# Other token blocks and the other operand standing in a two-product layer on Trainium2

## The chip, the cores and the metric

The kernel runs on one core of a Trainium2 chip. Its time is the device time of one execution, in microseconds (us); a version is judged by the median of several executions. The work of a core is done by TensorE (PE, matrix products, with PEld for its weight loads), VectorE (DVE), ScalarE (ACT), GpSimd (POOL) and SyncE (SP, whose queue issues the DMAs here).

## The reference

Attention with a cap on its scores, and then a layer of two matrix products with a gate between them:

```python
scores = cap * tanh(q @ k.T / sqrt(64) / cap)          # batch 4, 12 heads, 448 tokens, head size 64
attn   = softmax(scores);  x = attn @ v                # x: 1792 tokens x 768
h = x @ w_in                                           # 768 x 2048
g = h * cos(h)
out = g @ w_out                                        # 2048 x 768, out: 1792 x 768
```

## The kernel before

**Attention** runs in 12 cycles of three head pairs each, in an order written out by hand: a list of parts with due times (`PLAN`, a cycle of 13.8 us), sorted into one sequence. It leaves `x` in SBUF, split into a high and a low part (`xh`, `xl`, type fp32r), with the model dimension on the partitions and the tokens along the free axis. In its last cycle it already begins the layers: `BEGIN` places the first product of two units (`layers.begin`, into banks of the tile `pair`), and `layers.first` does most of the first unit's elementwise work there.

**The layers** are cut into 8 groups (`NGRP`) of 256 hidden columns, that is two units of 128 (`GF = 2`), and each group into 4 blocks of 448 tokens (`S`), one for each batch. A group and block is a step, 32 in all. Products are made of three terms, high x high, low x high and high x low, so 18 matmuls make a unit's first product (6 chunks of the model dimension, line 196: 128 columns of `w_in` stand, 448 tokens move). In the second product (line 601) 128 columns of `w_out` stand and 448 tokens of the gated values move: for each of the 6 chunks of output rows 2 units x 3 terms, 36 matmuls a block.

`Layers.step` is the written order of a step. On PE: both units' first products of this block, then the second product of the block before (`prev`), in three bank pairs; the first two come from the tile `pair` (two buffers of two banks), the third is `rest` (one buffer). On ACT and DVE: a piece of the weights of a later group is taken from 64-bit to fp32r words (`magnitude` on ACT; `clamp`, `shift`, `tail_bits`, `sign_bit` on DVE, lines 231 to 256; `high` on ACT and `low` on GpSimd in the next step); each unit passes through `turns` (ACT, 558), `whole_turns` (DVE, 561), `reduce` (two on DVE, 566 and 567), `cosine` (ACT, 570), `gate` (DVE, 573), `high` (ACT, 576) and `low` (DVE, 579); and the sums of `prev` are added from PSUM to `acc` in SBUF (DVE, 613; a copy in the first group, 611). The third chunk's addition is left to the next step (`older`). In the last group each addition is followed by its output DMA on SP's queue (616). The output leaves with the model dimension first, and the host transposes it.

Of the kernel before, what the change touches and what calls it, by code (L numbers as in the profile page):

```python
# [22 lines left out]
DM = H * D  # L23
DFF = 2048
KC = DM // 128
NF = DFF // 128
NG = 4
NQUAD = NPAIR // 2
# [46 lines left out]
EARLY = [2, 4, 6, 8]  # L75
EARLY_AT = dict(no_sign=2.4, scale=2.9, cap=3.4, shift=3.9, tail_bits=16.2, sign_bit=17.1, load=17.2, high=18.1, low=19.8, load_rest=20.0)
BUSY = 6, 5
PAD = 144
KD = 512
QK = KD + S  # L80
Q = slice(KD, QK)
# [23 lines left out]
@with_exitstack  # L105
def attention_moe(ctx: ExitStack, tc: tile.TileContext, qkv, cap, w_in, w_out, out):
    nc = tc.nc
    const = ctx.enter_context(tc.tile_pool(name="const", bufs=1))

    with tc.manual_schedule():  # L110
        busy = const.tile([128, 512], BF16, name="busy")
        nc.vector.memset(busy, 0.0)
        with tc.tile_pool(name="first", bufs=1, space=PSUM) as pool:
            keep_busy(nc, pool.tile([128, 512], F32, name="idle"), busy, BUSY[0])
        capt = const.tile([128, 1], F32, name="capt")
        nc.sync.dma_start(out=capt, in_=cap.rearrange("(a b) -> a b", b=1).to_broadcast([128, 1]))
        w64 = const.tile([128, DM, 2], I32, name="w64")
        u = const.tile([128, DM], I32, name="u")
        raw = w64.bitcast(F32).rearrange("p a b -> p (a b)")[:, 0:QK]
        for h in (slice(0, 64), slice(64, 128)):  # L120
            nc.sync.dma_start(out=raw[h], in_=qkv[0, h, 0:QK])
        second = const.tile([128, QK], F32, name="second")
        nc.sync.dma_start(out=second, in_=qkv[1, :, 0:QK])
        nc.sync.dma_start(out=u.bitcast(F32)[:, 0:RAW - QK], in_=qkv[0, :, QK:RAW])
        cabs = const.tile([128, PAD], F32, name="cabs")[:, 0:1]
        nc.scalar.activation(cabs, capt, AF.Abs)  # L126
        inv = const.tile([128, 1], F32, name="inv")
        nc.vector.reciprocal(inv, capt)
        nc.vector.tensor_scalar_mul(inv, inv, 1.0 / math.sqrt(D))
        bits = nc.values_load(cabs[0:1, 0:1].bitcast(I32))  # L130
        with tc.If(bits < CAP_LIMIT_BITS) as cmp:
            body(tc, w64, u, second, busy, qkv, capt, inv, w_in, w_out, out, True)
        with cmp.Else():
            body(tc, w64, u, second, busy, qkv, capt, inv, w_in, w_out, out, False)


def body(tc, w64, u, second, busy, qkv, capt, inv, w_in, w_out, out, bounded):
    with ExitStack() as ctx:
        xp = ctx.enter_context(tc.tile_pool(name="xp", bufs=1))
        xh = xp.tile([128, NPAIR, NT], F32R, name="xh")  # L140
        xl = xp.tile([128, NPAIR, NT], F32R, name="xl")
        wts = Weights(tc, w64, u, w_in, w_out)
        angles = xp.tile([128, 128], F32, name="angles")
        tc.nc.gpsimd.memset(angles[:, 0:1], math.pi / 2)
        tc.nc.gpsimd.memset(angles[:, 1:2], 0.25)
        wts.open_in(xp, (0, 1))
        wts.open_in(xp, (0,), "wo")
        banks = Banks(ctx.enter_context(tc.tile_pool(name="banks", bufs=2, space=PSUM)))
        keep_busy(tc.nc, banks.rest()[:, 1], busy, BUSY[1])
        layers = Layers(tc, banks, wts, xh, xl, angles, out)  # L150
        with ExitStack() as actx:
            if bounded:
                attention(actx, tc, banks, second, qkv, capt, inv, xh, xl, wts, layers, xp)
            else:
                attention_general(actx, tc, banks, qkv, capt, inv, xh, xl)
                for f in (0, 1):
                    wts.whole("wi", f)
                wts.whole("wo", 0)
                wts.load("wo", 1)
                wts.words()  # L160
                wts.load("wi", 2)
                for j in range(GF):
                    layers.begin(j)
                layers.sine()
        with ExitStack() as mctx:
            layers.open(mctx)
            layers.run()
# [21 lines left out]

def hidden(nc, wts, f, xh, xl, h, b):  # L190
    hi, lo = wts.get("wi", f)
    toks = slice(S * b, S * b + S)
    for k in range(KC):
        ks = slice(128 * k, 128 * k + 128)
        for i, (w, x) in enumerate(terms(f // GF, hi, lo, xh, xl)):
            nc.tensor.matmul(h[:, 0:S], lhsT=w[:, ks], rhs=x[:, k, toks],  # L196
                             start=(k == 0 and i == 0), stop=(k == KC - 1 and i == 2))


# [271 lines left out]
        eng.tensor_copy(out, in_)  # L471


def attention(ctx, tc, banks, second, qkv, capt, inv, xh, xl, wts, layers, pool):
    nc = tc.nc
    a = Heads(ctx, tc, banks, qkv, capt, inv, xh, xl, True)
    a.first(wts.w64.bitcast(F32).rearrange("p a b -> p (a b)")[:, 0:QK], second, wts.u.bitcast(F32)[:, 0:RAW - QK])
    a.fill()
    todo = []

# [6 lines left out]
    for j, time in enumerate(BEGIN):  # L487
        at(CYCLE * (NQ - 1) + time, lambda j=j: layers.begin(j))
    at(CYCLE * (NQ - 1) + FIRST, layers.sine)
    at(CYCLE * (NQ - 1) + FIRST, lambda: layers.first(pool))  # L490
    pieces = (("wi", 0), ("wi", 1), ("wo", 0), ("wo", 1), ("wi", 2))
    at(CYCLE + 4.0, lambda: wts.load(*pieces[0]))
    for i, cycle in enumerate(EARLY):
# [40 lines left out]
GF = 2  # L534
# [4 lines left out]
class Unit:  # L539


    def __init__(self, m, f, j, b):
        self.m, self.f, self.j, self.b = m, f, j, b
        self.h, self.gone = None, ()

    def product(self, bank=None):
        if self.h is None:
            h = bank if bank is not None else self.m.banks.single()
            hidden(self.m.nc, self.m.wts, self.f, self.m.xh, self.m.xl, h, self.b)
            self.h = h[:, 0:S]  # L550

    def tile(self, name):
        return self.pool.tile([128, S], F32, name=name, tag=name)

    def turns(self):
        m = self.m
# [16 lines left out]
        self.m.nc.vector.tensor_mul(self.y, self.h, self.y)  # L573

    def high(self):
        self.m.nc.scalar.copy(self.g[0][:, self.j], self.y)  # L576

    def low(self):
        self.m.nc.vector.tensor_sub(self.g[1][:, self.j], self.y, self.g[0][:, self.j])  # L579


class Block:


    def __init__(self, m, G, b, g):
        self.m, self.G, self.b, self.g = m, G, b, g
        self.y = {}

    def last(self, i):
        return self.G == NGRP - 1 and self.b == B - 1 and i == 2  # L590

    def product(self, i):
        m = self.m
        y = self.y[i] = m.banks.product(i)
        gh, gl = self.g
        for e in range(2):
            c = slice(128 * (2 * i + e), 128 * (2 * i + e) + 128)
            for j in range(GF):
                hi, lo = m.wts.get("wo", GF * self.G + j)
                for k, (w, x) in enumerate(terms(self.G, hi, lo, gh, gl)):  # L600
                    m.nc.tensor.matmul(y[:, e, 0:S], lhsT=w[:, c], rhs=x[:, j],  # L601
                                       start=(j == 0 and k == 0), stop=(j == GF - 1 and k == 2))

    def add(self, i):
        m, y = self.m, self.y.pop(i)
        toks = slice(S * self.b, S * self.b + S)
        parts = [slice(0, 1), slice(1, 2)] if self.last(i) else [slice(0, 2)]
        for e in parts:
            acc = m.acc[:, 2 * i + e.start:2 * i + e.stop, toks]
            if self.G == 0:  # L610
                m.nc.vector.tensor_copy(acc, y[:, e, 0:S])
            else:
                m.nc.vector.tensor_add(acc, y[:, e, 0:S], acc)  # L613
            if self.G == NGRP - 1:
                rows = m.out[128 * (2 * i + e.start):128 * (2 * i + e.stop), toks]
                m.nc.sync.dma_start(out=rows.rearrange("(e p) t -> p e t", p=128), in_=acc)


class Layers:
# [14 lines left out]
    def sine(self):  # L634
        self.nc.scalar.activation(self.angles[:, 2:3], self.angles[:, 1:2], AF.Sin)

    def first(self, pool):

        unit = self.begun[0]
        unit.pool, unit.gone = pool, ("turns", "whole_turns", "reduce", "cosine", "gate")  # L640
        for part in unit.gone:
            getattr(unit, part)()

    def open(self, ctx):
# [2 lines left out]
        accp = ctx.enter_context(self.tc.tile_pool(name="m_acc", bufs=1))  # L647
        self.wts.open_in(accp, (2, 3))
        self.wts.open_in(accp, (1, 2), "wo")
        self.acc = accp.tile([128, KC, NT], F32, name="acc")  # L650

    def run(self):
        prev, older = None, None
# [3 lines left out]
    def step(self, step, prev, older):  # L657
# [2 lines left out]
        piece = self.todo.pop(0) if self.todo else None  # L660
        units, cur = [], None
        if step < NSTEP:
            g = [self.gp.tile([128, GF, S], F32R, name=nm, tag=nm) for nm in ("gh", "gl")]
            units = [Unit(self, GF * G + j, j, b) for j in range(GF)] if step else self.begun
            for unit in units:
                unit.pool, unit.g = self.vp, g
# [8 lines left out]
                getattr(units[j], part)()  # L675

        def add(block, i):
            if block is not None:
                block.add(i)

        if self.done:
            wts.high(*self.done)
            wts.low(*self.done)
        on(0, "product")
        on(1, "product")
        if prev is not None:
            for i in range(3):
                prev.product(i)
        add(older, 2)
        on(0, "turns")  # L690
        w("magnitude")
        w("clamp")
        w("shift")
        on(0, "whole_turns")
        on(0, "reduce")
        on(0, "cosine")
        w("tail_bits")
        on(0, "gate")
        on(0, "high")
        w("sign_bit")  # L700
        on(1, "turns")
        on(0, "low")
        on(1, "whole_turns")
        on(1, "reduce")
        on(1, "cosine")
        add(prev, 0)
        on(1, "gate")
        on(1, "high")
        add(prev, 1)
        on(1, "low")  # L710
        if step == NSTEP:
            add(prev, 2)
        self.done = piece
        if self.todo and step:
            wts.load(*self.todo[0])
# [1 line left out]


_INS = ['qkv', 'cap', 'w_in', 'w_out']
_OUTS = [((DM, NT), 'float32')]  # L720


def _layout(inputs):
# [46 lines left out]
```

## Time and profile before

| | us |
|---|---|
| median of 3 runs (lowest, highest) | 664.13 (663.76, 664.15) |
| the profiled execution's own time | 664.33 |
| its span, first to last instruction | 662.5 |
| PE busy, share of the span | 651.9, 98% |
| DVE busy | 493.8, 75% |
| ACT busy | 318.1, 48% |
| POOL busy | 62.0, 9% |

The span is what the profile's rows cover; the profiled execution is 1.8 us longer than its span, and 0.20 us above the median. Rows of the timeline and of the chain count from the span's start. Records of matmuls overlap, so a matmul's record is longer than the time from its start to the next matmul's start.

### The profile page before, as it was taken

How to read it: one execution, taken by the hardware profiler on the slowest of the kernel's cores; microseconds unless marked ns; L12 is line 12 of the kernel's file. 1: busy time of each engine (PE TensorE's matmuls, PEld its weight loads, DVE VectorE, ACT ScalarE, POOL GpSimd, SP SyncE). 2: the span in 40 equal slices, each digit the busy share in tenths (PEclk: the TensorE clock that was granted, in tenths of full speed). 3: DMA queues.
4: the chain of work that ended last, by engine and by line, in shares of the span. 5: the costliest groups of instructions: out<-in, count | busy, mean ns of one | idle time of the engine just before them, and what ended most of it. 6: DMA issues, size and time to landing. Idle time of an engine off the chain costs nothing.

```text
span 662.5 us, 8791 instructions
## 1 busy us (share of the span) xinstructions
PE 651.9 (98%) x3563; PEld 490.0 (74%) x3563; DVE 493.8 (75%) x739; ACT 318.1 (48%) x385; POOL 62.0 (9%) x39
## 2 busy tenths in 40 slices
PE   7999999999999999999999999999999999999996
PEld 2333333333489999999999999999999999999995
DVE  1599999997778876677777776677777776677663
ACT  4999999999724433333333333333333333333220
POOL 0001011000011111111111111111111121111000
PEclk9899999999999999999999999999999999999998
DMA  7044332542001211111112111111112111110224
GB/s 257 10 151 147 111 139 92 182 150 102 1 1 50 94 49 47 48 47 48 48 52 85 55 47 48 48 48 49 48 57 72 63 48 48 48 48 0 84 85 171
DMA packets 19616, 49.41 MB, mean 75 GB/s; under 512 B 2160, under 2 KB 5232, under 8 KB 19568
## 3 DMA queue, kind: packets, MB, share of 16 engines
q1 hardware_dynamic: 19568, 48.77, 21.8%
q8 instruction: 30, 0.49, 0.3%
q14 instruction: 18, 0.15, 0.1%
HBM read 43.25 MB, written 5.51 MB: 74 GB/s over the span
## 4 chain that ended last, share of the span: by engine, by line
PE 98%; ACT 1%; DMA 0%; issue 0%; DVE 0%
PE single L196 35%; PE pair L601 24%; PE rest L601 12%; PE single L421 12%; PE pair L328 9%; PE rest L337 3%; PE rest L430 2%; PE pair L196 1%; DMA capt<-in_cap_dram 0%; PE rest L102 0%; ACT t L362 0%; ACT late L347 0%; ACT t L347 0%; DVE acc L613 0%; ACT cabs L126 0%
## 5 line engine op out<-in xcount | busy, mean ns | idle before, releaser
L570 ACT ACTIVATE y<-y,angles 128x448 f32<-128x448 f32 x64 | 43.0, 672 | 149.4 <-DVE y L567 149.4
L558 ACT ACTIVATE v<-single,angles 128x448 f32<-128x448 f32 x62 | 39.2, 633 | 101.4 <-PE single L196 101.4
L246 DVE TENSOR_SCALAR u<-u 128x768 f32<-128x768 f32 x28 | 15.7, 561 | 94.9 <-ACT u L231 94.9
L613 DVE TENSOR_TENSOR acc<-pair,acc 128x896 f32<-128x896 f32 x56 | 60.6, 1083 | 3.9 <-PE pair L601 3.9
L576 ACT CAST gh<-y 128x448 fp32r<-128x448 f32 x64 | 36.3, 567 | 49.6 <-DVE y L573 49.6
L328 PE MATMUL pair<-qk 64*128 64x448 f32 x264 | 58.6, 562 | 0.0
L328 PEld LDWEIGHTS pair<-qk 64*128 64x128 f32 x264 | 22.7, 186 | 36.2 <-issue 20.1
L347 ACT ACTIVATE t<-pair,inv 128x896 f32<-128x896 f32 x48 | 45.9, 1004 | 6.0 <-PE pair L328 5.5
L579 DVE TENSOR_TENSOR gl<-y,gh 128x448 fp32r<-128x448 f32 x64 | 40.8, 638 | 4.0 <-ACT gh L576 4.0
L362 ACT ACTIVATE t<-t,capt 128x1792 f32<-128x1792 f32 x24 | 42.8, 1783 | 0.4
L401 DVE TENSOR_TENSOR sum<-t 128x896 f32<-128x896 f32 x24 | 26.1, 1088 | 21.9 <-ACT t L362 21.9
L567 DVE SCALAR_TENSOR_TENSOR y<-v,y 128x448 f32<-128x448 f32 x64 | 40.0, 625 | 2.2
L421 PE MATMUL single<-late,v 128*32 128x448 f32 x368 | 40.7, 542 | 0.0
L573 DVE TENSOR_TENSOR y<-single,y 128x448 f32<-128x448 f32 x62 | 38.2, 616 | 2.7 <-ACT y L570 2.7
L566 DVE SCALAR_TENSOR_TENSOR y<-v,single 128x448 f32<-128x448 f32 x62 | 38.5, 621 | 2.1
L421 PE MATMUL single<-t,v 128*32 128x448 f32 x368 | 39.4, 547 | 0.0
L601 PE MATMUL pair<-gh,wo0h 128*128 128x448 f32 x96 | 35.3, 368 | 0.0
L601 PE MATMUL pair<-gh,wo0l 128*128 128x448 f32 x96 | 35.3, 368 | 0.0
L601 PE MATMUL pair<-gl,wo0h 128*128 128x448 f32 x96 | 35.3, 368 | 0.0
L196 PE MATMUL single<-xl,wi2h 128*128 128x448 f32 x96 | 35.3, 368 | 0.0
L196 PE MATMUL single<-xh,wi2h 128*128 128x448 f32 x96 | 35.3, 368 | 0.0
L196 PE MATMUL single<-xh,wi2l 128*128 128x448 f32 x96 | 35.3, 368 | 0.0
(143 smaller groups left out, 1609.5 us busy)
## 6 DMA issues: line engine op xcount, KB each, us to landing
w<-in_w_in_dram SPq DMA_DIRECT2D x32, 384.0 KB, 3.6
w<-in_w_out_dram SPq DMA_DIRECT2D x32, 384.0 KB, 3.6
qk<-in_qkv_dram SPq DMA_DIRECT2D x22, 480.0 KB, 5.5
v<-in_qkv_dram SPq DMA_DIRECT2D x23, 256.0 KB, 4.0
out_dram<-acc SPq DMA_DIRECT2D x11, 448.0 KB, 2.5
w<-in_qkv_dram SPq DMA_DIRECT2D x2, 240.0 KB, 3.8
second<-in_qkv_dram SPq DMA_DIRECT2D x1, 480.0 KB, 5.7
out_dram<-acc SPq DMA_DIRECT2D x2, 224.0 KB, 2.8
```

The source lines that it names most:

```text
L196: nc.tensor.matmul(h[:, 0:S], lhsT=w[:, ks], rhs=x[:, k, toks], start=(k == 0 and i == 0), stop=(k == KC - 1 and i == 2))
L328: self.nc.tensor.matmul(ps[:, h, 0:S], lhsT=x[mine, 128 * g:128 * g + 128], rhs=x[mine, Q], start=True, stop=True)
L347: self.nc.scalar.activation(out, ps[:, :, 0:S], AF.Tanh, scale=self.inv)
L362: self.nc.scalar.activation(t, t, AF.Exp, scale=self.capt)
L421: self.nc.tensor.matmul(self.acc[q][e][o], lhsT=self.v[q, a][:, g, d], rhs=t, start=(g == first), stop=(g == last), tile_position=(0, o.st ...
L558: m.nc.scalar.activation(self.v, self.h, AF.Identity, bias=m.quarter, scale=1.0 / (2.0 * math.pi))
L566: m.nc.vector.scalar_tensor_tensor(self.y, self.v, -TWO_PI_HI, self.h, op0=ALU.mult, op1=ALU.add)
L567: m.nc.vector.scalar_tensor_tensor(self.y, self.v, -TWO_PI_LO, self.y, op0=ALU.mult, op1=ALU.add)
L570: self.m.nc.scalar.activation(self.y, self.y, AF.Sin, bias=self.m.half_pi)
L579: self.m.nc.vector.tensor_sub(self.g[1][:, self.j], self.y, self.g[0][:, self.j])
L601: m.nc.tensor.matmul(y[:, e, 0:S], lhsT=w[:, c], rhs=x[:, j], start=(j == 0 and k == 0), stop=(j == GF - 1 and k == 2))
L613: m.nc.vector.tensor_add(acc, y[:, e, 0:S], acc)
```

## The change

Token blocks are 512, 512, 384 and 384 (starting at 0, 512, 1024, 1408) instead of four of 448. In the second product 128 tokens of the gated values stand and 384 of the 768 columns of `w_out` move, the two halves one after the other with the same standing operand; a bank pair holds 128 tokens x 768, so a block has 4 or 3 chunks, and the fourth takes a buffer of `pair` again. `acc` and the output have the tokens first, and the host's transpose goes. The order of additions in a step changes: `magnitude` goes ahead of the first unit's `turns`; the first chunk's addition moves from behind the second unit's cosine to behind the first unit's low part (in step 1 to before `tail_bits`); a fourth chunk's addition is left to the next step as the third's is; in step 0 the second unit's `turns` goes first. Tiles of a unit are 512 wide; the first unit's scratch is the tile `second`, now 1,024 wide, which held a piece of attention's input, and `PAD` shrinks by the same 64 words.

```diff
+HALF = DM // 2
+BLOCKS = 512, 512, 384, 384
+STARTS = 0, 512, 1024, 1408
+WIDE = max(BLOCKS)
-PAD = 144
+PAD = 80
...
-        second = const.tile([128, QK], F32, name="second")
-        nc.sync.dma_start(out=second, in_=qkv[1, :, 0:QK])
+        second = const.tile([128, 1024], F32, name="second")
+        nc.sync.dma_start(out=second[:, 0:QK], in_=qkv[1, :, 0:QK])
...
-    toks = slice(S * b, S * b + S)
+    n = BLOCKS[b]
+    toks = slice(STARTS[b], STARTS[b] + n)
...
-            nc.tensor.matmul(h[:, 0:S], lhsT=w[:, ks], rhs=x[:, k, toks],
+            nc.tensor.matmul(h[:, 0:n], lhsT=w[:, ks], rhs=x[:, k, toks],
...
     def tile(self, name):
-        return self.pool.tile([128, S], F32, name=name, tag=name)
+        t = self.space[name] if self.space else self.pool.tile([128, WIDE], F32, name=name, tag=name)
+        return t[:, 0:BLOCKS[self.b]]
...
     def product(self, i):
         m = self.m
         y = self.y[i] = m.banks.product(i)
+        toks = slice(128 * i, 128 * i + 128)
         gh, gl = self.g
-        for e in range(2):
-            c = slice(128 * (2 * i + e), 128 * (2 * i + e) + 128)
-            for j in range(GF):
-                hi, lo = m.wts.get("wo", GF * self.G + j)
-                for k, (w, x) in enumerate(terms(self.G, hi, lo, gh, gl)):
-                    m.nc.tensor.matmul(y[:, e, 0:S], lhsT=w[:, c], rhs=x[:, j],
+        for j in range(GF):
+            hi, lo = m.wts.get("wo", GF * self.G + j)
+            for k, (w, x) in enumerate(terms(self.G, hi, lo, gh, gl)):
+                for e in range(2):
+                    m.nc.tensor.matmul(y[:, e, 0:HALF], lhsT=x[:, j, toks], rhs=w[:, HALF * e:HALF * e + HALF],
                                        start=(j == 0 and k == 0), stop=(j == GF - 1 and k == 2))
...
     def add(self, i):
-        toks = slice(S * self.b, S * self.b + S)
+        t = STARTS[self.b] // 128 + i
...
-            acc = m.acc[:, 2 * i + e.start:2 * i + e.stop, toks]
+            acc = m.acc[:, t, e]
...
-                rows = m.out[128 * (2 * i + e.start):128 * (2 * i + e.stop), toks]
-                m.nc.sync.dma_start(out=rows.rearrange("(e p) t -> p e t", p=128), in_=acc)
+                cols = slice(HALF * e.start, HALF * e.stop)
+                m.nc.sync.dma_start(out=m.out[128 * t:128 * t + 128, cols],
+                                    in_=acc.rearrange("p e n -> p (e n)"))
...
+        if step == 0:
+            units[1].turns()
+            units[1].gone = ("turns",)
...
         if prev is not None:
-            for i in range(3):
+            for i in range(prev.count):
                 prev.product(i)
         add(older, 2)
+        add(older, 3)
+        w("magnitude")
         on(0, "turns")
-        w("magnitude")
         w("clamp")
         w("shift")
         on(0, "whole_turns")
         on(0, "reduce")
         on(0, "cosine")
+        if step == 1:
+            add(prev, 0)
         w("tail_bits")
         on(0, "gate")
         on(0, "high")
         w("sign_bit")
         on(1, "turns")
         on(0, "low")
+        if step != 1:
+            add(prev, 0)
         on(1, "whole_turns")
         on(1, "reduce")
         on(1, "cosine")
-        add(prev, 0)
         on(1, "gate")
         on(1, "high")
         add(prev, 1)
         on(1, "low")
         if step == NSTEP:
             add(prev, 2)
+            add(prev, 3)
...
-    return _np.ascontiguousarray(got[0].T)
+    return got[0]
```

## Rows read from the trace of the kernel before

**Rows 1.** The page: busy time of PE, and the chain that ended last.

```profile
PE 651.9 (98%) x3563; PEld 490.0 (74%) x3563; DVE 493.8 (75%) x739; ACT 318.1 (48%) x385; POOL 62.0 (9%) x39
...
PE 98%; ACT 1%; DMA 0%; issue 0%; DVE 0%
```

**Rows 2.** The chain in order of time (start, length, what): begun units, one step.

```profile
175.63 3.83 PE pair L196 x18
...
183.36 3.91 PE pair L196 x18
...
440.24 7.44 PE single L196 x36
447.68 4.96 PE pair L601 x24
452.63 2.48 PE rest L601 x12
```

**Rows 3.** Windows, the layers stage: busy time of each engine, then granted clock, DMA.

```profile
187.10:655.80 468.70, 468.70 (x2269) 425.49 (x2267) 344.01 (x525) 158.59 (x247) 53.55 (x29) 1.00 0.17 56
```

**Rows 4.** Timeline (start, length, engine, line, operation): one matmul and load.

```profile
400.39 0.37 PE L196 MATMUL single<-xl,wi3h 128*128 128x448 f32 x1
400.40 0.19 PEld L196 LDWEIGHTS single<-xh,wi3h 128*128 128x128 f32 x1
```

**Rows 5.** Timeline of loads in attention, first and last of six groups.

```profile
103.10 0.13 PEld L421 LDWEIGHTS single<-t,v 128*32 128x32 f32 x4 [0.25 <-issue]
...
104.98 0.13 PEld L421 LDWEIGHTS single<-t,v 128*32 128x32 f32 x4 [0.24 <-issue]
```

**Rows 6.** Timeline of the first begun unit, loads, then matmuls.

```profile
175.56 0.19 PEld L196 LDWEIGHTS pair<-xh,wi0h 128*128 128x128 f32 x1 [0.73 <-ACT late L347]
175.67 0.19 PEld L196 LDWEIGHTS pair<-xh,wi0l 128*128 128x128 f32 x1
...
175.56 0.47 PE L196 MATMUL pair<-xh,wi0h 128*128 128x448 f32 x1
175.87 0.36 PE L196 MATMUL pair<-xh,wi0l 128*128 128x448 f32 x1
...
179.11 0.36 PE L196 MATMUL pair<-xl,wi0h 128*128 128x448 f32 x1
```

**Rows 7.** Busy-work at the start: group of all loads, then two in the timeline.

```profile
L102 PEld LDWEIGHTS <-busy 128*128 128x128 bf16 x11 | 1.4, 134 | 4.9 <-issue 3.7 <-DVE busy L112 1.2
...
1.59 0.15 PEld L102 LDWEIGHTS <-busy 128*128 128x128 bf16 x1 [0.28 <-issue]
...
2.87 0.15 PEld L102 LDWEIGHTS <-busy 128*128 128x128 bf16 x1 [0.28 <-issue]
```

**Rows 8.** Timeline of ACT and DVE in the step of rows 2.

```profile
444.53 0.88 ACT L231 ACTIVATE u<-w 128x768 f32<-128x768 f32 x1
445.44 0.56 DVE L246 TENSOR_SCALAR u<-u 128x768 f32<-128x768 f32 x1 [3.62 <-ACT u L231]
...
446.51 0.39 DVE L561 TENSOR_SCALAR v<-v 128x448 f32<-128x448 f32 x1
446.94 0.62 DVE L566 SCALAR_TENSOR_TENSOR y<-v,single 128x448 f32<-128x448 f32 x1
...
448.13 0.95 DVE L252 SCALAR_TENSOR_TENSOR u<-w,u 128x768 int32<-128x768 int32 x1
...
452.55 1.08 DVE L613 TENSOR_TENSOR acc<-pair,acc 128x896 f32<-128x896 f32 x1
```

**Rows 9.** Timeline: block 0's last low part, and the matmul that reads it.

```profile
194.69 0.63 DVE L579 TENSOR_TENSOR gl<-y,gh 128x448 fp32r<-128x448 f32 x1 [0.63 <-ACT gh L576]
...
195.59 0.37 PE L601 MATMUL pair<-gl,wo1h 128*128 128x448 f32 x1
```

**Rows 10.** Timeline of the end: last matmul, last additions.

```profile
655.63 0.37 PE L601 MATMUL rest<-gh,wo0l 128*128 128x448 f32 x1
656.03 1.16 DVE L613 TENSOR_TENSOR acc<-rest,acc 128x448 f32<-128x448 f32 x2 [1.39 <-PE rest L601]
```

More of the change, by code (lines that the diff above doesn't have):

```diff
@@ L152, in body @@
             if bounded:
-                attention(actx, tc, banks, second, qkv, capt, inv, xh, xl, wts, layers, xp)
+                attention(actx, tc, banks, second, qkv, capt, inv, xh, xl, wts, layers)
             else:
@@ L471, in copy, with attention @@
         eng.tensor_copy(out, in_)
-def attention(ctx, tc, banks, second, qkv, capt, inv, xh, xl, wts, layers, pool):
+def attention(ctx, tc, banks, second, qkv, capt, inv, xh, xl, wts, layers):
     nc = tc.nc
     a = Heads(ctx, tc, banks, qkv, capt, inv, xh, xl, True)
-    a.first(wts.w64.bitcast(F32).rearrange("p a b -> p (a b)")[:, 0:QK], second, wts.u.bitcast(F32)[:, 0:RAW - QK])
+    a.first(wts.w64.bitcast(F32).rearrange("p a b -> p (a b)")[:, 0:QK], second[:, 0:QK], wts.u.bitcast(F32)[:, 0:RAW - QK])
     a.fill()
@@ L489, in attention @@
     at(CYCLE * (NQ - 1) + FIRST, layers.sine)
-    at(CYCLE * (NQ - 1) + FIRST, lambda: layers.first(pool))
+    at(CYCLE * (NQ - 1) + FIRST, lambda: layers.first(second))
     pieces = (("wi", 0), ("wi", 1), ("wo", 0), ("wo", 1), ("wi", 2))
@@ L543, in __init__ @@
         self.m, self.f, self.j, self.b = m, f, j, b
-        self.h, self.gone = None, ()
+        self.h, self.gone, self.space = None, (), None
     def product(self, bank=None):
@@ L549, in product, with result @@
             hidden(self.m.nc, self.m.wts, self.f, self.m.xh, self.m.xl, h, self.b)
-            self.h = h[:, 0:S]
+            self.h = h[:, 0:BLOCKS[self.b]]
     def tile(self, name):
-        return self.pool.tile([128, S], F32, name=name, tag=name)
+        t = self.space[name] if self.space else self.pool.tile([128, WIDE], F32, name=name, tag=name)
+        return t[:, 0:BLOCKS[self.b]]
+    def result(self, part):
+        return self.g[part][:, self.j, 0:BLOCKS[self.b]]
     def turns(self):
@@ L575, in high @@
     def high(self):
-        self.m.nc.scalar.copy(self.g[0][:, self.j], self.y)
+        self.m.nc.scalar.copy(self.result(0), self.y)
     def low(self):
-        self.m.nc.vector.tensor_sub(self.g[1][:, self.j], self.y, self.g[0][:, self.j])
+        self.m.nc.vector.tensor_sub(self.result(1), self.y, self.result(0))
 class Block:
@@ L587, in __init__ @@
         self.y = {}
+        self.count = BLOCKS[b] // 128
     def last(self, i):
-        return self.G == NGRP - 1 and self.b == B - 1 and i == 2
+        return self.G == NGRP - 1 and self.b == B - 1 and i == self.count - 1
     def product(self, i):
@@ L605, in add @@
         m, y = self.m, self.y.pop(i)
-        toks = slice(S * self.b, S * self.b + S)
+        t = STARTS[self.b] // 128 + i
         parts = [slice(0, 1), slice(1, 2)] if self.last(i) else [slice(0, 2)]
         for e in parts:
-            acc = m.acc[:, 2 * i + e.start:2 * i + e.stop, toks]
+            acc = m.acc[:, t, e]
             if self.G == 0:
-                m.nc.vector.tensor_copy(acc, y[:, e, 0:S])
+                m.nc.vector.tensor_copy(acc, y[:, e, 0:HALF])
             else:
-                m.nc.vector.tensor_add(acc, y[:, e, 0:S], acc)
+                m.nc.vector.tensor_add(acc, y[:, e, 0:HALF], acc)
             if self.G == NGRP - 1:
-                rows = m.out[128 * (2 * i + e.start):128 * (2 * i + e.stop), toks]
-                m.nc.sync.dma_start(out=rows.rearrange("(e p) t -> p e t", p=128), in_=acc)
+                cols = slice(HALF * e.start, HALF * e.stop)
+                m.nc.sync.dma_start(out=m.out[128 * t:128 * t + 128, cols],
+                                    in_=acc.rearrange("p e n -> p (e n)"))
 class Layers:
@@ L635, in sine, with first @@
         self.nc.scalar.activation(self.angles[:, 2:3], self.angles[:, 1:2], AF.Sin)
-    def first(self, pool):
+    def first(self, space):
         unit = self.begun[0]
-        unit.pool, unit.gone = pool, ("turns", "whole_turns", "reduce", "cosine", "gate")
+        unit.space = {"v": space[:, 0:WIDE], "y": space[:, WIDE:2 * WIDE]}
+        unit.gone = ("turns", "whole_turns", "reduce", "cosine", "gate")
         for part in unit.gone:
@@ L649, in open @@
         self.wts.open_in(accp, (1, 2), "wo")
-        self.acc = accp.tile([128, KC, NT], F32, name="acc")
+        self.acc = accp.tile([128, NT // 128, 2, HALF], F32, name="acc")
     def run(self):
@@ L662, in step @@
         if step < NSTEP:
-            g = [self.gp.tile([128, GF, S], F32R, name=nm, tag=nm) for nm in ("gh", "gl")]
+            g = [self.gp.tile([128, GF, WIDE], F32R, name=nm, tag=nm) for nm in ("gh", "gl")]
             units = [Unit(self, GF * G + j, j, b) for j in range(GF)] if step else self.begun
@@ L677, in add @@
         def add(block, i):
-            if block is not None:
+            if block is not None and i < block.count:
                 block.add(i)
+        if step == 0:
+            units[1].turns()
+            units[1].gone = ("turns",)
         if self.done:
@@ L719 @@
 _INS = ['qkv', 'cap', 'w_in', 'w_out']
-_OUTS = [((DM, NT), 'float32')]
+_OUTS = [((NT, DM), 'float32')]
 def _layout(inputs):
```

## Prediction

> **What bounds the kernel now.** I read the page first. TensorE (PE) is busy for 98% of the span, and the chain that ended last is 98% PE. VectorE (DVE) has 75%, ScalarE (ACT) 48% [rows 1]. Busy PE alone proves little, since matmul records overlap, so I asked the chain in order of time. In the layers, one step repeats exactly: 36 matmuls of the first product in 7.44 us, 24 plus 12 of the second in 4.96 and 2.48, then the next step, with nothing between [rows 2]. A step is 14.88 us for 72 matmuls, 206.7 ns each, and over the whole layers stage (187.1 to 655.8, granted clock 1.00) 468.7 us stand for 2,268 starts, again 206.7 [rows 3]. So PE never waits there, and the time of this stage is (number of matmuls) x (time from one start to the next).
>
> The timeline of single matmuls says what those 206.7 ns are [rows 4]. At clock 1.00 (2.4 GHz) 448 columns stream in 448 / 2.4 = 186.7 ns, so each matmul carries 20.0 ns beyond its columns. A weight load of 0.19 us begins with the matmul before it, and every matmul has its own load.
>
> **The change part by part.**
>
> *Columns.* The first product has 16 x 18 matmuls for each block, before and after; its columns are 288 x 1,792 = 516,096 either way. The second had 8 x 4 x 36 = 1,152 matmuls of 448 columns, and now has 14 token chunks x 8 x 12 = 1,344 of 384. That is 516,096 columns again, 215.0 us of streaming for each product. Nothing is saved or added in streaming; only the 20.0 ns can change the sum.
>
> *The extra as a fixed amount.* With 20.0 ns per matmul, 512 columns take 233.3 ns and 384 take 180.0. First product: 576 x 233.3 + 576 x 180.0 = 238.1 us, as now (1,152 x 206.7 = 238.1). Second: 1,344 x 180.0 = 241.9, against 238.1. The change costs 192 x 20.0 ns = **+3.84 us**. For the first product this holds for any amount that is linear in the columns, because the blocks average 448.
>
> What could the extra be instead? The trace holds fp32r only at 448 columns, so I bound it. Full-precision products, two records each, show a group every 0.376 us (1.88 us for five) [rows 5]; 2 x 448 columns at 2.4 GHz are 373.3, so the fixed part there is 2.7 ns. If only 2.7 ns is fixed, the 192 extra matmuls cost 0.5 us. From the other side, nothing shows a fixed part above 20.0. The one place where fp32r matmuls are closer is the unit begun inside attention: from 175.87 to 179.11 sixteen matmuls start 202.5 ns apart, 15.8 over their columns [rows 6]; the next such unit is back at about 206.7 (its 18 matmuls take 3.91 us against 3.83 in the chain [rows 2]). If all 2,496 matmuls took the 15.8, the sum would be 39.4 us instead of 46.1, which is 6.6 below today. I take the fixed 20.0: it holds for both products, with either operand standing, whatever DVE, ACT and DMA do beside it.
>
> The Trainium skill has a rule that speaks against my reading: its page "TensorE: Matmul & The Clock Gate", section "Back-to-back issue gap", gives an isolated gap of N / 2.4 + 2.5 ns, so 189.2 ns for 448 columns. The trace does not agree (206.7). By that rule the 192 extra matmuls would cost an estimated 0.5 us and the change could not be told from none.
>
> *Weight loads.* There are 192 more. A load's record is 0.19 us [rows 4] and a 384-column matmul streams for 0.160, so I asked whether a load could become the pace. The unit begun in attention answers [rows 6]: after idle, load and matmul start together at 175.56, the second load starts 0.11 us later, and the first matmul's record is only 0.10 to 0.11 longer than those behind it. Weights are usable about 0.11 us after their load starts, not after the 0.19 of the record, and 0.11 is under 0.160. Cost taken: 0; the other end is a rival.
>
> *The same tokens standing twice.* The two halves of w_out follow each other with the same standing operand. The busy-work matmuls at the start use one standing operand throughout, and each still has a load of its own, 11 for 6 + 5 matmuls, three periods in 1.28 us [rows 7]. I count every second load in full.
>
> *Other engines.* DVE's work is the same number of columns: for a unit 0.39 and four of 0.62, 2.87 us at 448; for a piece of weights two of 0.56 and two of 0.95, 3.02 [rows 8]. Additions go from 12 of 1.08 us to 14 of about 0.93 (768 columns for 896) in four steps, +0.1 us. Steps become 14.88, 17.04, 15.12 and 12.96 us instead of 14.88 each. The tightest is the last: 3.0 + 2 x 2.5 + 4 x 0.93 = 11.7 us of DVE in 12.96. What runs over is made up in the next two. It costs PE nothing as long as the low parts are ready when PE has done the next step's units, 6.5 to 8.4 us later.
>
> *The new wait.* A 512 block has a fourth chunk, which takes the bank pair of the first, so that must be added while chunks 1 and 2 run (4.32 us). Queued ahead of it on DVE are the older additions, clamp, shift and unit 0's chain to its low part. With unit 0 done 4.4 us into the step, that chain at 512 columns (the 448-column rows and up to 0.07 for 64 more, since 448 further columns take an addition from 0.58 to 1.08 [rows 8, 10]: 0.70 ACT, 0.42, 1.4, 0.74 ACT, 0.70, sign bits 0.95, 0.70) ends near 10.0. The first chunk is done at 10.7, its addition at 11.7, and PE needs the bank at 14.9. Today magnitude sits behind turns on ACT and holds clamp to 445.44, 5.2 us into its step [rows 2, 8]; moved ahead, it frees DVE earlier. Price 0; without that cover each microsecond late is paid 16 times.
>
> *The ends.* Begun units of 512 columns take 0.96 us more in attention's tail, where PE has no gap to hide it, and give it back in the short blocks. Block 0's second product then needs its low part near 198.3; today it is ready at 195.32 against a need at 195.59 [rows 9]. A unit 1 that is 0.96 later and 0.6 of wider operations bring it to about 197.3 at worst: no stall. At the other end the addition of chunk 0 now stands before unit 1's chain, so the last block's low part comes about 14.0 us into a step of 12.96, with PE's need at 14.04 (chunk 0 done 8.8, add 0.9, unit 1's chain of 2.4 to its cosine, gate, addition 1 and low behind it): 0 to 0.5 us, I take 0.1. The last two additions are 384 wide for 448, 1.02 us for 1.16 [rows 10]: -0.15. The last output DMA goes out of the same place with an eighth less data; I count nothing for it, since nothing shows a price by size.
>
> *Sum.* +3.84 - 0.15 + 0.1 = +3.8 us on the profiled 664.33, which stands 0.20 above the median of 664.13: 668.1 there, **667.9** as a median.
>
> **Rivals.**
>
> *Faster: the second matmul of a pair does not pay.* If the extra comes from bringing in different weights, the second half, whose standing operand is already there, would pay the 2.7 ns of [rows 5]. That takes 17.3 ns off 672 matmuls, 11.6 us: **656.3**. It turns the sign from 5.7 ns (3.8 / 672). Against it: loads are issued for repeated operands too [rows 7]. For it: those rows are bf16 at 1.2 GHz (512 columns in 0.427 us, nothing over), so they can't show its price in fp32r. Chance 0.14. The same page of the Trainium skill, section "Step-by-step: what each phase is for", says that one load can serve many matmuls; no row here shows a matmul without one.
>
> *Faster: the extra falls to the 15.8 ns* of the begun unit [rows 6]: -6.6 us, **657.5**. One unit of 64 shows it; chance 0.09.
>
> *No change: the extra grows with the columns.* 2.7 fixed and 17.3 x 384 / 448 = 14.8 make 177.5 ns, 1,344 of them 238.6 us, +0.5: **664.6**. All fp32r rows have one width, so nothing excludes it; against it, a slower stream would not have shown the 202.5 of [rows 6]. Chance 0.12.
>
> *Much slower: the load's whole record sets a floor*: 0.19 us and some 0.02 to the next matmul would be the 206.7 ns. Then 1,344 x 26.7 ns = +35.8 us over my forecast in the second product, 512 columns take 213.3 + 2.7 = 216.0 and the short ones 206.7, +5.4 in the first: **709**. That 0.19 and 186.7 ns lie so close lets it live, and [rows 6] speak against it. Chance 0.07.
>
> **How the numbers follow.** The forecast keeps 0.58, with a range of its own from 666.5 to 669 (last-step stall, tail). Within 0.2%, 1.3 us, is about what a measurement here can tell from no change. Faster: 0.14 + 0.09 = 0.23; same 0.12; slower 0.58 + 0.07 = 0.65. The range from 656 to 670 takes in the bounds 2.7 to 20.0 and both faster cases, and leaves out the floor and some edges, under 0.2.
>
> **What would show it.** Right: fp32r starts 233 ns apart at 512 columns and 180 at 384, both of a pair alike, the step 14.88, 17.04, 15.12, 12.96, and no wait of PE for DVE. Wrong: 163 for a pair's second half, 177 at 384 with 236 at 512, 207 at 384, or PE waiting for additions before a fourth chunk.

## The result

The changed kernel takes 652.45 us (median of 4, 651.99 to 653.35) against 664.14 (median of 4) for the kernel before: a ratio of 0.9827, with a 95% interval from 0.981 to 0.9844. It is 1.7% faster. Forecast was 667.9, slower, in a range from 656 to 670; the result lies outside the range and on the other side.

The page of the changed kernel: busy time and instructions of each engine, and the chain that ended last, by engine. They answer to [rows 1].

```profile
PE 640.2 (98%) x3755; PEld 498.3 (76%) x3755; DVE 501.7 (77%) x755; ACT 320.0 (49%) x385; POOL 62.1 (10%) x39
...
PE 93%; DVE 3%; ACT 1%; issue 1%; DMA 0%; POOL 0%; ACTq 0%
```

There are 192 matmuls more, as counted, each with a load of its own (3,755 of both), and still PE is busy for 11.7 us less. The chain in order of time (start, length, what) over a round of blocks says where that is; it answers to [rows 2].

```profile
522.07 8.20 PE single L201 x36
530.27 4.18 PE pair L611 x24
534.45 2.08 PE rest L611 x12
536.53 8.20 PE single L201 x36
...
551.00 2.08 PE pair L611 x12
553.08 6.24 PE single L201 x36
...
567.64 6.24 PE single L201 x36
```

The four steps take 14.46, 16.55, 14.56 and 12.48 us (the last from the next round's start at 580.12), where 14.88, 17.04, 15.12 and 12.96 were forecast. Nothing stands between the pieces, left out or shown; each is shorter. A chunk of 12 matmuls of 384 columns takes 2.08 us, 173.3 ns each, not 180.0; 36 of 512 take 8.20, some 227 ns each, not 233.3. Both widths now carry 13.3 ns over their columns instead of 20.0. In single records of the first product (the timeline), the starts are 0.227 apart:

```profile
528.75 0.39 PE L201 MATMUL single<-xh,wi1h 128*128 128x512 f32 x1
528.97 0.39 PE L201 MATMUL single<-xh,wi1l 128*128 128x512 f32 x1
529.20 0.39 PE L201 MATMUL single<-xl,wi1h 128*128 128x512 f32 x1
```

2,496 matmuls times 6.7 ns are 16.6 us under the forecast. Only little is lost again. PE's one wait in the layers is 0.3 us, for the addition that frees a fourth chunk's bank pair in step 2 (waits of PE: engine and line, what it waited for, total us, times, longest):

```profile
PE pair L611 <- DVE acc L621: 0.3, 1, 0.3
```

### The profile page after: what moved, and what is told of

Same layout as the page of the kernel before. It is cut to its first block, busy times and chain, and to the rows that moved or that the text cites. A ratio compares the mean times of both kernels' runs of the same rounds, so it can differ in the third digit from the quotient of the medians.

```text
span 651.5 us, 9197 instructions
## 1 busy us (share of the span) xinstructions
PE 640.2 (98%) x3755; PEld 498.3 (76%) x3755; DVE 501.7 (77%) x755; ACT 320.0 (49%) x385; POOL 62.1 (10%) x39
## 4 chain that ended last, share of the span: by engine, by line
PE 93%; DVE 3%; ACT 1%; issue 1%; DMA 0%; POOL 0%; ACTq 0%
PE single L201 32%; PE pair L611 24%; PE single L426 12%; PE rest L611 10%; PE pair L333 9%; PE rest L342 3%; PE rest L435 2%; PE pair L201 1%; DVE gl L588 1%; DMA capt<-in_cap_dram 0%; DVE acc L621 0%; DVE y L575 0%; DVE y L582 0%; PE rest L106 0%; POOL wi2l L269 0%
## 5 line engine op out<-in xcount | busy, mean ns | idle before, releaser
L579 ACT ACTIVATE y<-y,angles 128x384 f32<-128x384 f32 (+1 forms) x63 | 42.3, 671 | 161.5 <-DVE y L576 161.5
L623 DVE TENSOR_TENSOR acc<-pair,acc 128x768 f32<-128x768 f32 x70 | 66.7, 953 | 14.3 <-PE pair L611 14.2
L585 ACT CAST gh<-y 128x384 fp32r<-128x384 f32 (+1 forms) x63 | 35.8, 567 | 45.6 <-DVE y L582 45.6
L582 DVE TENSOR_TENSOR y<-single,y 128x384 f32<-128x384 f32 (+1 forms) x62 | 38.5, 621 | 25.4 <-ACT y L579 25.4
L567 ACT ACTIVATE v<-single,angles 128x384 f32<-128x384 f32 (+1 forms) x62 | 39.0, 629 | 29.0 <-PE single L201 28.9
L576 DVE SCALAR_TENSOR_TENSOR y<-v,y 128x384 f32<-128x384 f32 (+1 forms) x63 | 39.3, 624 | 2.2
L588 DVE TENSOR_TENSOR gl<-y,gh 128x384 fp32r<-128x384 f32 (+1 forms) x63 | 38.8, 616 | 2.5 <-ACT gh L585 2.5
L575 DVE SCALAR_TENSOR_TENSOR y<-v,single 128x384 f32<-128x384 f32 (+1 forms) x62 | 38.4, 619 | 2.1
L201 PE MATMUL single<-xh,wi2l 128*128 128x512 f32 (+1 forms) x96 | 34.9, 363 | 0.0
L201 PE MATMUL single<-xh,wi2h 128*128 128x512 f32 (+1 forms) x96 | 34.8, 363 | 0.0
```

What stands on the lines that cost most here:

```text
L201: nc.tensor.matmul(h[:, 0:n], lhsT=w[:, ks], rhs=x[:, k, toks], start=(k == 0 and i == 0), stop=(k == KC - 1 and i == 2))
L567: m.nc.scalar.activation(self.v, self.h, AF.Identity, bias=m.quarter, scale=1.0 / (2.0 * math.pi))
L576: m.nc.vector.scalar_tensor_tensor(self.y, self.v, -TWO_PI_LO, self.y, op0=ALU.mult, op1=ALU.add)
L579: self.m.nc.scalar.activation(self.y, self.y, AF.Sin, bias=self.m.half_pi)
L588: self.m.nc.vector.tensor_sub(self.result(1), self.y, self.result(0))
L623: m.nc.vector.tensor_add(acc, y[:, e, 0:HALF], acc)
```

## The experiments

Why 13.3 ns and not 20.0? I held three theories of the missing 6.7 ns: A, the number of columns sets it; B, the place in memory of the moving slice; C, a standing operand that is used twice. Each run is told with what I expected of it. The two kernels without layers, the one with shifted tiles and the one with 24 matmuls of 384 columns ran once each; the others are medians of 4 or 10 executions.

**Matmuls alone.** No attention and no layer: stretches of 48 fp32r matmuls, with other widths, first columns and standing operands. The list, name by name (columns, first moving column, step between moving slices, first standing column, its step):

```python
("n512", 512, 0, 2048, 0, 128) ... n448, n384, n480, n416, n496, n432, n320, n256
("m448", 448, 448, 2048, 0, 128), ("m384", 384, 448, ...), ("m512", 512, 448, ...)
("o448", 448, 64, 2048, 0, 128), ("o384", 384, 64, ...)
("w448", 448, 0, 2048, 64, 128), ("w384", ...)      # standing slices elsewhere
("s448", 448, 0, 2048, 0, 0), ("s384", ...)         # one standing operand throughout
("f448", 448, 0, 0, 0, 128)                         # one moving slice throughout
("p448", 448, 0, 1792, 0, 128), ("p384", ...)
("r448", 448, 0, 2048, 0, 128)                      # n448 once more
```

> No layer at all: 23 stretches of 48 fp32r matmuls, each of one width, one first column and one choice of standing operand; the output is not the reference's. Theory A (the extra per matmul is set by the number of columns that move): 384 and 512 columns start 173.3 and 226.7 ns apart (13.3 over the columns), 448 starts 206.7 apart (20.0), whatever the first column and whatever stands. Theory B (it is set by where in memory the moving slice begins): 448 from column 0 goes to 200.0, and 384 or 512 from column 448 take 20.0 over their columns. Theory C (a repeated standing operand is cheap): the stretches with one standing operand go to 2.7 ns over their columns, 189.4 and 162.7. If A, the widths 480, 416, 496, 432, 320, 256 show which widths pay 13.3 and which 20.

The chain of this kernel joins stretches whose name differs only in its digits:

```profile
140.61 18.05 PE o L53 x96
158.66 18.24 PE w L53 x96
176.90 18.24 PE s L53 x96
195.14 9.91 PE f L53 x48
205.05 18.25 PE p L53 x96
223.30 9.93 PE r L53 x48
```

48 matmuls of 384 columns at 173.3 ns are 8.32 us. So 448 columns take 9.92 us, 206.7 ns each, in w, s, p and r, and 9.73, 202.7, in o. The groups by shape (busy us, mean ns of one record) show it without any sum; a record here is 161 to 163 ns longer than the spacing of starts:

```profile
L53 PE MATMUL s<-x,w 128*128 128x448 f32 x48 | 10.1, 368 | 0.0
...
L53 PE MATMUL n<-x,w 128*128 128x448 f32 x48 | 9.9, 365 | 0.0
...
L53 PE MATMUL s<-x,w 128*128 128x384 f32 x48 | 8.5, 334 | 0.0
...
L53 PE MATMUL n<-x,w 128*128 128x256 f32 x48 | 5.9, 283 | 0.0
```

C falls: one standing operand throughout (s) gives 206.7 and 173.3, the same as six different ones. B falls: 384 columns have 173.3 from column 0, 64 or 448, with either step. A holds for all widths but one. Taking the mean spacing of the last 39 starts of each stretch, the time over the columns is 13.3 ns at 256, 320, 384 and 512, 15.0 at 416, 15.9 at 432, 16.8 at 480 and 16.7 at 496. At 448 there are two paces, 16.0 and 20.0: n and r are one and the same stretch, and show one of them each. The kernel before runs at the slower of the two, which carries more over its columns than any other width of this list.

**The blocks alone.** Blocks of 512, 512, 384, 384, with the second product and the order of additions as before:

```diff
-                    m.nc.tensor.matmul(y[:, e, 0:S], lhsT=w[:, c], rhs=x[:, j],
+                    m.nc.tensor.matmul(y[:, e, 0:self.n], lhsT=w[:, c], rhs=x[:, j, 0:self.n],
```

> Blocks of 512, 512, 384, 384, but the second product as before (128 columns of w_out stand, 512 or 384 tokens move) and the order of additions as before. Theory A: all 2,304 matmuls take 13.3 ns over their columns, 15.4 us less than before, about 649, and 2.6 us less than the changed kernel (192 matmuls fewer) if no wait is added. Theory C (the pairs are what gains): the first product alone decides, and it gains nothing from pairs, so about 664.

649.46 us, ratio 0.9785 (0.976 to 0.9811): theory A, to half a microsecond. In its chain the second product of a 512 block (24 + 12 matmuls) and of a 384 block:

```profile
441.76 5.48 PE pair L611 x24
447.24 2.72 PE rest L611 x12
449.96 6.26 PE single L201 x36
456.23 4.16 PE pair L611 x24
460.39 2.08 PE rest L611 x12
```

The widths alone give the gain. The other operand standing is not a part of it; it costs its 192 matmuls, which is 2.6 us at 13.3 ns. This version is also the fastest of the study, 3.0 us under the changed kernel.

**Halves apart.** In the changed kernel, the loop over the halves of w_out goes outside:

```diff
+        for e in range(2):
             for j in range(GF):
...
-                for e in range(2):
```

> The changed kernel with the two halves of w_out one after the other as whole chains, so no standing operand is used twice in a row. Theory A: no change, 384 columns stay at 173.3 ns, 652.5. Theory C: matmuls of the second product go from 173.3 to 180, and the time up by up to 9 us.

653.03 us, ratio to the kernel before 0.9844 (0.9825 to 0.9863). A chunk without pairs is as fast as one with them:

```profile
548.60 2.08 PE rest L611 x12
550.68 2.08 PE pair L611 x12
```

**All later tiles 256 bytes lower**, in the kernel before: `PAD = 144` becomes `PAD = 80`.

> The kernel before with PAD at 80 for 144, so that all later tiles lie 256 bytes lower. Theory A: 448 columns stay at 206.7 ns, time 664. Theory B: the extra moves away from 20.0, by up to 6.7 ns on 2,304 matmuls, up to 15 us less.

664.46 us, and a step's first product is 7.44 us as in [rows 2]. No run speaks for B.

```profile
440.63 7.44 PE single L196 x36
```

**Two paces of 448 columns.** Stretches again without layers, each entered from another width:

```python
("a512", 512, 24), ("a448", 448, 400), ("b384", 384, 24), ("b448", 448, 100), ("c512", 512, 6), ("c448", 448, 100),
("d320", 320, 24), ("d448", 448, 48), ("e480", 480, 24), ("e448", 448, 48),
("g192", 192, 48), g128, g288, g352, g400, g464, g504, g508, ("h512", 512, 48)
```

> No layer: stretches of fp32r matmuls of one width after another; the output is not the reference's. In the first such kernel 448 columns ran at two paces, 202.7 ns in three stretches that followed 512 or 256 columns, and 206.7 in five that followed 384 or a stretch already at 206.7. Theory A1 (the pace of 448 depends on how the stretch is entered and then holds): 448 after 512 stays at 202.7 for all 400 matmuls, after 384 it is 206.7 for all 100, after only six of 512 it is 202.7 again. Theory A2 (the pace drifts, or follows the address): the 400 fall to 206.7 on the way, or the three stretches have one pace. The other widths: if only multiples of 64 settle at 13.3 over the columns, 192 and 128 show it and 288, 352, 400, 464, 504, 508 lie between 14.5 and 17.

```profile
30.21 86.51 PE a L48 x424
116.72 24.85 PE b L48 x124
141.57 22.05 PE c L48 x106
163.61 13.25 PE d L48 x72
176.86 15.11 PE e L48 x72
```

a is 24 x 226.7 and then 400 at 202.7 ns (5.44 + 81.07 = 86.51): the pace holds for all 400. b is 24 at 174.5 on average (173.4 once they have settled) and then 100 at 206.7. After 320 it is 202.6, after 480 it is 206.7. But c, after six matmuls of 512, is 206.7, so the width before is not the whole rule; those six were not yet at 226.7 (starts 223 to 237 ns apart). The other widths: 13.3 ns over the columns at 352 and 400 too, so it is not only multiples of 64; 11.7 at 288, 15.5 at 464, 16.7 at 504, 15.8 at 508. So 504 columns start as far apart as 512 do (226.7 ns). The single starts tell the two paces of 448 apart: at the slower one all stand 206 or 207 ns apart, at the faster one 199, 207, 203, 202 and 203, over and over. Short ones meet another bound: 192 and 128 columns have one pace, 111.7 ns, and the same record. That lies near the 0.11 us that the prediction read for a load from [rows 6], but no run shows what sets it.

```profile
L48 PE MATMUL g<-x,w 128*128 128x192 f32 x48 | 5.5, 274 | 0.0
L48 PE MATMUL g<-x,w 128*128 128x128 f32 x48 | 5.5, 274 | 0.0
```

**The other pace in the kernel before.** Matmuls of 512 or 384 columns, result unused, go ahead of step 1's first product:

```diff
+        if step == 1:
+            other = self.banks.rest()[:, 0]
+            for _ in range(6):
+                nc.tensor.matmul(other, lhsT=wts.get("wi", 0)[0][:, 0:128], rhs=self.xh[:, 0, 0:512], start=True, stop=True)
```

> The kernel before, with six matmuls of 512 columns (1.36 us, their result unused) ahead of step 1's first product. Theory A1: the layers' 2,268 matmuls of 448 columns enter at 202.7 ns and keep it: 9.1 us less and 1.4 more, about 656.4. Theory A2 or any cause in memory layout or other engines: 206.7 stays, about 665.

> The same with six matmuls of 384 columns (1.04 us). Theory A1: entered from 384 the pace is 206.7, about 665. If the six matmuls alone help by moving the start, it falls like the one with 512 columns.

664.89 (ratio 1.0006, 0.9981 to 1.003) and 665.0 us (1.0007, 0.9979 to 1.0034): six change nothing, and my expectation for 512 missed by 8.5 us. Stretch c, which ran in the same set, shows the same: behind six of 512 the pace is the slower one. So I put in 24 (`range(24)`):

> The kernel before with 24 matmuls of 512 columns (5.4 us, result unused) ahead of step 1's first product, for the six that changed nothing. In the kernel without layers 448 columns after six of 512 ran at 206.7 ns, and after 24, which had settled at 226.7, at 202.7 for all 400. Theory A1 (the pace of 448 is fixed by what it is entered from, and holds): 202.7 in the layers, 9.1 us less and 5.4 more, about 660.4. Theory A2 (in the kernel it is drawn back to 206.7): 669.5.

> The same with 24 matmuls of 384 columns (4.2 us). Theory A1, by the stretch of 100 that followed 24 of 384: 206.7 stays, about 668.3. If the delay alone moves the pace, it is as with 512.

660.98 us, ratio 0.9958 (0.9944 to 0.9971), with 24 of 512, and 667.74 in one execution with 24 of 384. In the chain a step of the first is 14.59 us instead of 14.88; the second stays at [rows 2]. First the kernel with 24 of 512:

```profile
440.88 7.30 PE single L196 x36
448.18 4.86 PE pair L601 x24
453.04 2.43 PE rest L601 x12
```

Then the one with 24 of 384:

```profile
443.65 7.44 PE single L196 x36
```

Over 32 steps, with other engines at work beside it, the pace that was entered held: 2,268 starts in 459.4 us, 202.7 ns each. The same matmuls, on the same data in the same places, get faster behind 5.4 us of useless work, while 1.0, 1.4 and 4.2 us of other useless work leave them as they were. So the pace hangs on what PE ran before, and not on the data, its place or a delay as such. What keeps it is not shown.

**Other widths in the blocks.** The blocks alone once more, as 480, 480, 416, 416:

```diff
-BLOCKS = 512, 512, 384, 384
-STARTS = 0, 512, 1024, 1408
+BLOCKS = 480, 480, 416, 416
+STARTS = 0, 480, 960, 1376
```

> Blocks of 480, 480, 416, 416 with the second product as before (w_out stands): same matmuls, same columns and same order as with 512, 512, 384, 384. Theory A (the width sets the extra): 480 at 216.8 ns and 416 at 188.3, as without layers, 1,152 x (216.8 + 188.3 - 226.7 - 173.3) = +5.9 us against 649.5, about 655. Theory D (unequal blocks, the wider tiles or their places gain, not the width): about 649.5.

653.60 us, ratio to the kernel before 0.9844 (0.9828 to 0.9861), 4.1 over the 649.46 of the other run. It is the width that costs. The expectation stood 1.8 us higher because it took settled spacings: over all starts of the layers, 512 and 384 columns take 227.5 and 173.9 ns in the run with the blocks alone, since the first matmuls behind a change of width stand wider apart, and 480 and 416 take 216.8 and 188.0 here. 1,152 x (216.8 + 188.0 - 227.5 - 173.9) is 3.9 us. The same number of matmuls over the same columns, two steps' first products:

```profile
404.00 7.80 PE single L201 x36
...
434.22 6.79 PE single L201 x36
```

36 of 480 take 216.7 ns each and 36 of 416 take 188.6, within 0.5 ns of what they take alone.

**The old order.** The changed kernel, with the additions, magnitude and first turns where they were:

```diff
-        w("magnitude")
         on(0, "turns")
+        w("magnitude")
...
-        if step == 1:
-            add(prev, 0)
...
-        if step != 1:
-            add(prev, 0)
         on(1, "whole_turns")
         on(1, "reduce")
         on(1, "cosine")
+        add(prev, 0)
```

> The changed kernel with the order of additions, of magnitude and of the first turns as before. If the order is the cover that a fourth chunk needs: the first chunk's addition ends near 14.4 us of a 512-column step (clamp at 5.9, unit 0's chain, unit 1's chain to its cosine), when PE wants the bank pair at 14.4 (8.16 of units and three chunks of 2.08); PE waits 0.2 to 0.5 us in each of 16 blocks, 3 to 8 us more, 655.5 to 660. If the cover is not needed: within 1 us of 652.5.

656.89 us, ratio 0.988 (0.9817 to 0.9942), 4.4 over the changed kernel; its four executions (655.87 to 657.22) all lie above the four of the changed kernel (651.99 to 653.35). The sum fell into the expected range, but not for the expected reason. There are no 16 waits of 0.2 to 0.5 us: six times a start in a fourth chunk comes 0.06 us late. There is one wait, in step 1, behind attention (waits of PE, then windows with PE, PEld, DVE, ACT, POOL and granted clock):

```profile
PE pair L611 <- DVE acc L621: 3.3, 1, 3.3
```

```profile
200.00:206.60 6.60, 3.29 (x19) 2.96 (x18) 6.53 (x11) 2.98 (x6) 0.00 (x0) 1.00 0.37 119
206.60:209.90 3.30, 3.30 (x13) 3.30 (x12) 2.44 (x4) 0.54 (x1) 1.83 (x1) 0.50 0.00 0
```

Behind the wait the granted clock is 0.50 for 3.3 us (1.2 GHz), and 384 columns start 0.320 us apart, the columns alone and nothing over:

```profile
208.29 0.53 PE L201 MATMUL single<-xh,wi0l 128*128 128x384 f32 x1
208.61 0.53 PE L201 MATMUL single<-xl,wi0h 128*128 128x384 f32 x1
```

Ten matmuls or so at 0.147 us more are 1.5 us; with the wait itself, and less the 0.6 that the changed kernel loses in step 2, they make 4.2 of the 4.4. Which of the moved parts covers step 1 was not separated.

## Why the prediction was wrong

*Columns* was right: 516,096 for each product, and 192 matmuls more. *What bounds the kernel* was right: PE sets the time, so that number times spacing is the time.

*The extra as a fixed amount* failed, at the sentence "I take the fixed 20.0". That 192 more matmuls cost something was right: 2.6 us of the 3.0 between the changed kernel and the blocks alone, at 13.3 ns each. But 20.0 ns was one pace of one width, the only width of fp32r that the trace held. At 384 and 512 columns it is 13.3. In the sum, 2,496 matmuls at 13.3 are 33.3 us instead of 49.9, 16.6 less; settling at each change of width and the two small waits cost 1.8 in the layers, of which 0.1 was in the forecast. 668.1 - 16.6 + 1.7 = 653.2, and the profiled execution took 653.35.

The claim beside it, that the first product can't change because its blocks average 448, rested on an amount linear in the columns. It is not: 416, 432, 448, 480 and 496 all pay more than 384 and 512 on either side. The bounds were too narrow for the same reason. The begun unit of [rows 6] stood 4 ns closer than all others, with the same shapes, and I gave it a chance of 0.09 as an oddity of one unit. It was the other pace of 448 columns: its starts repeat 199, 207, 202, 203 and 202 ns, as in stretch a. Two spacings for one shape should have said that 20.0 is not a constant of a matmul; the rival that lets the extra fall deserved a far larger chance, though its 15.8 ns and 657.5 us were still too high. Of the other rivals, the pair whose second matmul is cheap fell with C, and an extra that grows with the columns fell with 384 and 512, which carry the same 13.3.

The Trainium skill (page "TensorE: Matmul & The Clock Gate", section "Back-to-back issue gap") gives N / 2.4 + 2.5 ns as the gap of an isolated matmul at the full clock. In these streams no fp32r width agrees with it; the smallest amount over the columns was 11.7. Its N / 1.2 for the slower clock agrees with the 0.320 us that 384 columns take behind the wait of the old order.

*Weight loads* was right: the 0.19 us of a load's record are no floor, since 256 columns follow at 120.0 ns. *The same tokens standing twice* was right too: a second matmul with the same operand standing is no cheaper (s384, and halves apart).

*The new wait* was right in its price, nearly nothing, but not in all of its reason: PE waits once, 0.3 us, in step 2, where I saw 3 us of slack in a step that starts on time. DVE does not start it on time: the changed kernel's chain in order of time leaves PE behind attention, and runs through DVE, ACT and GpSimd until that addition lets PE go on.

```profile
189.68 1.92 DVE gl L588
...
207.94 1.86 POOL wi2l L269
...
216.95 2.37 PE pair L611 x12
```

"Each microsecond late is paid 16 times" was wrong; without the cover a long wait comes once, in step 1, and the halved clock adds to it.

*The ends*: the last step lost 0.2 us instead of 0.1. The last additions take 1.02 us as worked out (the timeline's last of DVE), but from their start to the end of the span it is 6.9 us, against 6.5 in [rows 10]. The last output DMAs, 192 KB, land in 3.9 us where 224 KB took 2.8 (the pages' DMA issues). That longer tail is not shown to be the change's: with the same ends it is 6.2 us with the halves apart and 5.8 with the old order.

```profile
644.65 1.02 DVE L623 TENSOR_TENSOR acc<-rest,acc 128x384 f32<-128x384 f32 x2 [1.13 <-PE rest L611]
```

Why 448 columns have two paces, and why 512 is back at 13.3 when 504 and 508 are not, stays open. The widths other than 384, 448 and 512 were entered in one to three ways only, so a second pace of theirs is not excluded. What sets which of the two is entered is also known only in part: after settled stretches of 512, 320 and 256 it was the faster, after 384, 480 and six of 512 the slower.

## What to carry to other kernels

Where one width fills a trace, the time from start to start of a matmul is known for that width alone; before costing another tiling, measure its width by itself, in one kernel of short stretches. Here 256, 320, 352, 384, 400 and 512 columns of fp32r carried 13.3 ns each, but a narrow matmul has fewer columns to share it: one column costs 0.443 ns at 512, 0.451 at 384, 0.461 at the slower pace of 448 and 0.469 at 256. Going from 448 to 512 and 384 was worth 2% with the same matmuls. A reordering that looks like cover for every step may matter mostly in the first, where an engine still works off the stage before.

## What the runs showed of the hardware

- An fp32r matmul with its own load of 128 x 128 took 13.3 ns over its columns at 256, 320, 352, 384, 400 and 512, 11.7 at 288, and 15 to 20 at the other widths tried from 416 to 508, at the full clock. At half clock 384 columns had nothing over (0.320 us).
- 448 columns ran at 202.7 or 206.7 ns. The pace held for 400 matmuls alone and 2,268 in the kernel, and 24 unneeded matmuls of 512 columns ahead moved the whole kernel from one to the other.
- With 192 and with 128 columns the pace was 111.7 ns: there the columns no longer set it. 504 columns took as long as 512 (226.7 ns).
